# A planner that knows the turns in a product's banks, sums from copies, and another order of 104 products

## The chip, the cores and the metric

The kernel runs on one core of a Trainium2 chip. The metric is the device time of one execution in microseconds (us). The engines that matter are TensorE (PE in the profile, with PEld for its weight loads), VectorE (DVE), ScalarE (ACT) and the queue of SyncE (SP), which issues all DMAs. Each engine works through its own instructions strictly in order and waits for the others at semaphores.

## The reference

Sigmoid attention is followed by a two-layer MLP, all in float32:

```python
scores = scale * (q @ k^T) - log(S)          # batch 8, heads 12, S = 448, head_dim 64
x = merge_heads(sigmoid(scores) @ v)         # 3584 tokens x 768
h = x @ w_in                                 # 768 -> 2048
g = h * sigmoid(1.702 * h)
out = g @ w_out                              # 2048 -> 768
```

The two weight matrices arrive as float64 and are turned into float32 on the chip.

## The kernel before, in words

**Attention.** Two heads make a pair; 24 groups of two pairs are worked through one after the other. TensorE makes the scores (`sc`), ScalarE their sigmoid (`a`), TensorE the product with v (`av`), and `to_x` copies the result (tile `x32`) and stores it to DRAM (`xd`). Beside that, 16 pieces of the weights are decoded (`decode`, tiles `w32`) on VectorE and ScalarE.

**The MLP.** Both layers are computed by a bilinear scheme with 26 products of blocks in place of 32. There are two halves of the tokens (q = 0 and 1) and two layers (m = 0 and 1), so there are 4 x 26 = 104 products. For each one:

- VectorE adds and subtracts blocks of weights (`ws`, `wf`, `kw`) and blocks of x or g (`xs`, `kx`, `gs`, `kg`). These are the sums that the lists `W_SUMS`, `X_SUMS` and `G_SUMS` name.
- Each sum is split in two float32r parts, so that three matmuls give float32 precision. The upper part is a cast that ScalarE or VectorE makes, and the lower part is a subtraction that only VectorE makes (`split_piece` for the weights, tile `w_0` or `w_1`; `pair_of` for x and g, tiles `xp` and `gp`).
- TensorE runs 36 matmuls of 128x128x448 into the four banks of the tile `p{m}_{q}_{r}` (`products`). Products go to the bank groups `h0` and `h1` in turn, so a product's banks must be read out before the product after the next one can start.
- The product is added into up to several sums of products (`Net`): `h` for layer 0 (128 x 1792), `o` for layer 1 (128 x 1344). `Net.add` makes the additions, on VectorE; `Net.copied` makes the first copy of a sum on ScalarE or VectorE. A product can also start from a sum that ScalarE has copied into its banks ahead of the matmuls ("seeded"; `Net.seeds`, in `Net.product`), which saves the addition. ScalarE makes the activation of h (`gelu`).

**The order.** `SEQUENCE` is a table written out by hand: 104 entries (q, m, r). `ways` derives from it and from `AGAIN` how the piece of weights for each product is had: "made" by VectorE, "loaded" again from DRAM (`w<-c`), or the "same" as for one of the last two. `Plan.run` then plays all tasks through with a cost for each, and writes the instructions of every engine in the order in which they begin there. `since` is the time from which a task may begin; `SOON` and `PATIENCE` let an engine wait for a more urgent task; `HORIZON`, `URGENT`, `SPARE` and `KEEP` ration the buffers; `BACKLOG` and `PRESSING` hold DMAs back while the queue is long. These numbers decide only the order of instructions on each engine. On the chip the semaphores decide when they run.

**The turns.** A product's banks may not be read by VectorE and ScalarE at the same time. So where one engine's read stands behind the other's in the program, it waits for a semaphore of the other, although neither needs the other's result. `Plan.run` does not know of these waits.

Of the kernel before, what the change touches and what calls it, by code (L numbers as in the profile page):

```python
# [71 lines left out]
KEEP_FOR = dict(
    w0={0: 6, 1: 25, 2: 25, 3: 3, 4: 3, 5: 12, 6: 3, 7: 6, 8: 12, 9: 3, 10: 12, 13: 3, 14: 25, 15: 6, 16: 25, 17: 6, 18: 25, 19: 6, 20: 12, 21: 12, 22: 12, 24: 12, 25: 25},
    w1={0: 12, 1: 12, 2: 3, 3: 6, 4: 25, 5: 12, 6: 6, 8: 12, 9: 12, 10: 25, 11: 3, 13: 25, 15: 3, 17: 12, 18: 25, 19: 6, 20: 3, 21: 3, 22: 6, 23: 3, 24: 3, 25: 6},
    x0={0: 12, 1: 3, 2: 6, 3: 3, 4: 3, 5: 25, 7: 3, 8: 25, 9: 3, 10: 12, 12: 6, 13: 6, 14: 12, 15: 6, 16: 12, 17: 3, 20: 3, 23: 25, 24: 3},
    x1={0: 25, 1: 3, 2: 12, 3: 6, 5: 6, 6: 6, 7: 6, 8: 12, 10: 25, 11: 25, 12: 12, 13: 6, 14: 25, 15: 12, 16: 12, 17: 6, 18: 3, 19: 6, 20: 6, 21: 12, 22: 3, 24: 6, 25: 3},
    g0={0: 12, 1: 25, 2: 12, 4: 12, 5: 25, 6: 12, 8: 6, 9: 12, 10: 3, 11: 3, 12: 3, 13: 12, 14: 6, 15: 25, 16: 25, 17: 3, 18: 12, 20: 3, 21: 12, 22: 6, 23: 6, 24: 3, 25: 25, 26: 25, 29: 3, 30: 6, 31: 3, 32: 25, 35: 12, 37: 6, 38: 6, 39: 12, 40: 25, 41: 6, 42: 25},
    g1={0: 25, 1: 3, 2: 25, 3: 12, 4: 25, 5: 12, 6: 12, 7: 25, 8: 3, 9: 12, 11: 3, 12: 6, 13: 12, 14: 6, 15: 25, 16: 12, 17: 3, 18: 6, 19: 12, 20: 3, 21: 6, 22: 12, 23: 12, 24: 6, 25: 12, 26: 12, 27: 3, 28: 25, 29: 3, 30: 12, 31: 25, 32: 6, 33: 25, 34: 3, 35: 6, 36: 25, 37: 12, 38: 12, 39: 12, 40: 3, 41: 3, 43: 6},
# [1234 lines left out]
```

## Time and profile before

| | us |
|---|---|
| median of 3 runs (1034.95 to 1041.19) | 1035.44 |
| the profiled execution | 1035.04 |
| its span, first to last instruction | 1033.3 |

| engine | busy us | share of the span | instructions |
|---|---|---|---|
| PE (matmuls) | 1018.3 | 99% | 5588 |
| PEld (weight loads) | 832.3 | 81% | 5588 |
| DVE | 933.0 | 90% | 654 |
| ACT | 588.3 | 57% | 473 |

The granted TensorE clock is 1.0 throughout. The DMAs move 310.63 MB. The busy time of PE overlaps with itself (a matmul begins before the one ahead has ended), so that 99% does not mean that no time is lost there; the lost time is read from the waits and from the distance of the first to the last matmul. In the rows of waits, `DVE h L1262 <- ACT h L1228` says that VectorE's instruction of line 1262 (which writes a tile h) stood idle until ScalarE's instruction of line 1228 was done.

### The profile page before, as it was taken

The page shows a single profiled execution, that of the slowest core. Times are in us where ns is not written, and L with a number is a line of the kernel's source. Part 1 is how long each engine was busy: PE and PEld are TensorE (multiplying, and loading weights), DVE is VectorE, ACT ScalarE, POOL GpSimd, SP SyncE. Part 2 cuts the span into 40 slices and gives each one's busy share as a digit, 9 for nine tenths or more (in the row PEclk, how much of TensorE's full clock was granted, in tenths as well). Part 3 has the DMA queues.
Part 4 walks back from the last instruction along what each step waited for, and adds up shares of the span by engine and source line. Part 5 has one row for each costly group of instructions (what it writes and reads, how often), then busy time and mean ns, then how long its engine had stood idle before and what let it go on. Part 6 is the DMA issues. An engine that isn't in the chain of part 4 may idle for free.

```text
span 1033.3 us, 13713 instructions
## 1 busy us (share of the span) xinstructions
PE 1018.3 (99%) x5588; PEld 832.3 (81%) x5588; DVE 933.0 (90%) x654; ACT 588.3 (57%) x473; POOL 0.2 (0%) x4
## 2 busy tenths in 40 slices
PE   9999999999999999999999999999999999999998
PEld 5545454545898988898899999899999999999987
DVE  6998888897899988998899798999999999999896
ACT  6888887785364455545535444654654336454553
POOL 0000000000000000000000000000000000000000
PEclk9999999999999999999999999999999999999999
DMA  9999998878879868897988885875859389856755
GB/s 351 367 343 383 335 346 317 308 294 308 321 290 379 357 269 292 338 365 286 361 336 312 289 304 202 346 291 195 319 183 382 133 316 367 295 201 240 269 210 223
DMA packets 62799, 310.63 MB, mean 301 GB/s; under 512 B 6544, under 2 KB 14864, under 8 KB 58896
## 3 DMA queue, kind: packets, MB, share of 16 engines
q1 hardware_dynamic: 62736, 309.75, 79.8%
q8 instruction: 44, 0.72, 0.3%
q14 instruction: 19, 0.16, 0.0%
HBM read 200.38 MB, written 109.35 MB: 300 GB/s over the span
## 4 chain that ended last, share of the span: by engine, by line
PE 46%; DVE 4%; ACT 1%; issue 1%; DVEq 0%; ACTq 0%
PE p L845 46%; DVE gp L1052 1%; DVE o L1262 1%; DVE w L813 1%; DVE kg L788 1%; DVE h L1262 0%; ACT p L1186 0%; DVE x L788 0%; DVE h L1229 0%; DVE wf L788 0%; ACT h L1228 0%; ACT o L1228 0%; DVE gp L1041 0%; ACT o L1116 0%; DVEq L813 0%
## 5 line engine op out<-in xcount | busy, mean ns | idle before, releaser
L845 PE MATMUL p<-xp,w 128*128 128x448 f32 x1872 | 387.1, 367 | 8.8 <-DVE xp L1052 3.5
L845 PEld LDWEIGHTS p<-xp,w 128*128 128x128 f32 x1872 | 349.8, 188 | 46.1 <-DVE xp L1052 7.3
L845 PE MATMUL p<-gp,w 128*128 128x448 f32 x1872 | 380.9, 365 | 0.8 <-DVE w L813 0.8
L845 PEld LDWEIGHTS p<-gp,w 128*128 128x128 f32 x1872 | 351.2, 188 | 29.9 <-issue 1.4
L635 ACT ACTIVATE a<-sc,bias 128x896 f32<-128x896 f32 x168 | 156.1, 1014 | 42.9 <-PE sc L665 27.3
L680 PE MATMUL av<-a,vraw 128*64 128x448 f32 x576 | 113.5, 543 | 0.0
L1228 ACT COPY h<-p 128x1792 f32<-128x1792 f32 x30 | 49.7, 1658 | 105.2 <-PE p L845 50.8
L1228 ACT COPY o<-p 128x1344 f32<-128x1344 f32 x37 | 47.2, 1284 | 97.0 <-PE p L845 91.1
L1262 DVE TENSOR_TENSOR h<-h,p 128x1792 f32<-128x1792 f32 x40 | 79.8, 2017 | 20.7 <-ACT h L1228 18.2
L649 PEld LDWEIGHTS sc<-qk 64*128 64x128 f32 x846 | 75.6, 184 | 27.6 <-PE sc L665 16.2
L649 PE MATMUL sc<-qk 64*128 64x448 f32 x846 | 94.6, 373 | 0.8 <-DVE x L710 0.8
L680 PEld LDWEIGHTS av<-a,vraw 128*64 128x64 f32 x576 | 39.2, 137 | 63.2 <-issue 46.9
L1089 ACT ACTIVATE h<-h 128x1792 f32<-128x1792 f32 x28 | 47.4, 1702 | 15.3 <-DVE h L1262 15.3
L1262 DVE TENSOR_TENSOR o<-o,p 128x1344 f32<-128x1344 f32 x34 | 52.2, 1549 | 3.0 <-PE p L845 1.6
L519 DVE TENSOR_TENSOR qk<-qkraw,qk 128x896 fp32r<-128x896 f32 x47 | 50.7, 1089 | 0.6
L1052 DVE TENSOR_TENSOR xp<-x,xp 128x1344 fp32r<-128x1344 f32 x26 | 40.4, 1553 | 7.7 <-ACT xp L1040 7.5
L710 DVE COPY x<-av 128x896 f32<-128x896 f32 x23 | 25.1, 1091 | 17.2 <-PE av L693 17.1
L1052 DVE TENSOR_TENSOR gp<-gs,gp 128x1792 fp32r<-128x1792 f32 x19 | 38.4, 2022 | 1.7 <-ACT gp L1040 1.4
L1052 DVE TENSOR_TENSOR gp<-kg,gp 128x1792 fp32r<-128x1792 f32 x18 | 36.4, 2022 | 1.3 <-ACT gp L1040 1.2
L514 DVE CAST qk<-qkraw 128x896 fp32r<-128x896 f32 x37 | 22.9, 623 | 12.7 <-DMA qkraw<-qk 6.4
L813 DVE TENSOR_TENSOR w<-ws,w 128x1536 fp32r<-128x1536 f32 x19 | 33.3, 1753 | 0.8 <-ACT w L810 0.6
L813 DVE TENSOR_TENSOR w<-kw,w 128x1536 fp32r<-128x1536 f32 x18 | 31.6, 1753 | 2.7 <-ACT w L810 2.6
(109 smaller groups left out, 932.2 us busy)
## 6 DMA issues: line engine op xcount, KB each, us to landing
w<-c SPq DMA_DIRECT2D x34, 768.0 KB, 5.8
w<-w SPq DMA_DIRECT2D x16, 1536.0 KB, 10.5
kg<-kg SPq DMA_DIRECT2D x27, 896.0 KB, 7.0
gl<-g SPq DMA_DIRECT2D x26, 896.0 KB, 7.4
x<-xd SPq DMA_DIRECT2D x34, 672.0 KB, 7.2
c<-w SPq DMA_DIRECT2D x14, 1536.0 KB, 7.3
qkraw<-qk SPq DMA_DIRECT2D x47, 448.0 KB, 7.0
kw<-kw SPq DMA_DIRECT2D x25, 768.0 KB, 7.6
```

What stands on the lines that cost most here:

```text
L514: (costs[1], lambda: nc.vector.tensor_copy(hi(), src())),
L519: lambda: nc.vector.tensor_tensor(lo(), src(), hi().bitcast(F32), op=ALU.subtract),
L635: nc.scalar.activation(a.tile, ps.tile[:, :, :S], AF.Sigmoid, bias=bias, scale=scale)
L649: nc.tensor.matmul(ps.tile[:, j, :S], lhsT=src[kk][rows, S + c * P : S + (c + 1) * P], rhs=src[qq][rows, :S], start=i == 0, stop=i == len( ...
L680: nc.tensor.matmul(ps.tile[cols, n % 2, :S], lhsT=vr.tile[:, at : at + D], rhs=a.tile[:, j], start=c == 0, stop=False, skip_group_check=True,)
L710: (1.09, lambda: nc.vector.tensor_copy(xb.tile, ps.tile[:, :, :S])), [t], [xb, ps], rows)
L813: t_lo = task("DVE", dve(n), lambda: nc.vector.tensor_tensor(into()[:, :, 1], src(), into()[:, :, 0].bitcast(F32), op=ALU.subtract), [t_hi ...
L845: nc.tensor.matmul(ps, lhsT=ws(c // 6)[:, a, c % 6 * P : (c % 6 + 1) * P], rhs=x[:, d, k], start=start and i == 0 and j == 0, stop=stop an ...
L1052: nc.vector.tensor_tensor(part(1)(), node.view(), part(0)().bitcast(F32), op=ALU.subtract)
L1089: t = task("ACT", act(GB), lambda: nc.scalar.activation(view(), node.view(), AF.Gelu_apprx_sigmoid, scale=float(sign)), [*node.done, *(nod ...
L1228: t = on_either((act(self.n), lambda: nc.scalar.copy(view(), node.view())), (dve(self.n), lambda: nc.vector.tensor_copy(view(), node.view())),
L1262: nc.vector.tensor_tensor(view(), x.view(), y.view(), op=ALU.add if s0 == s else ALU.subtract)
```

## The change

It has four parts.

1. `Plan.run` learns of the turns: each task keeps the banks that it reads (`t.banks`), each bank its last reading engine and when that ends, and `since` holds a task back while the other engine reads there.
2. `COPIED` lists products that are copied out of their banks once (on ScalarE or VectorE), after which the additions read the copy.
3. `PLAIN` lists products that are no longer seeded or chained onto a sum in the banks. They begin with an empty bank, and are added by VectorE instead.
4. Another `SEQUENCE`, `AGAIN` and `KEEP_FOR`, and other numbers for the planner.

```diff
-SOON, PATIENCE = 6, 0.8
+SOON, PATIENCE = 4, 0.2
-HORIZON, URGENT, SPARE, KEEP = 14, 4, 1, 2
+HORIZON, URGENT, SPARE, KEEP = 22, 3, 1, 4
-BACKLOG, PRESSING = 6.0, 4
+BACKLOG, PRESSING = 1.0, 4
-ISSUE, LANDING, PER_KB, MM = 0.43, (2.2, 2.5), 0.0027, 0.203
+ISSUE, LANDING, PER_KB, MM = 0.43, (2.2, 3.0), 0.0027, 0.203
 SEQUENCE = (
-    (0, 0, 17), (0, 0, 18), (0, 0, 24), (1, 0, 13), (0, 0, 13), (1, 0, 2), (0, 0, 2), (0, 0, 6),
+    (0, 0, 8), (0, 0, 18), (0, 0, 10), (1, 0, 10), (0, 0, 13), (1, 0, 13), (0, 0, 2), (0, 0, 25),
...
+COPIED = ((0, 1, 2, 4, 6, 8, 13, 14, 16, 17, 18, 20, 21, 22, 23, 24,), ...
+PLAIN = ((0, 3, 5, 6, 8, 12, 13, 15, 16, 19, 21, 24, 25,), ...
...
+        for tag in ("h0", "h1"):
+            for b in self.rings[tag]:
+                for t in b.users if not b.apart else ():
+                    t.banks.append(b)
...
-        def since(t):
+        def since(t, e):
             when = t.ready
+            for b in t.banks:
+                if b.reader not in (None, e):
+                    when = max(when, b.read + SIGNAL)
...
                 free[e] = end - OVERLAP[e]
+                for b in t.banks:
+                    b.reader, b.read = e, max(b.read, end)
...
-                    if c < RANK and len(self.parents[c]) == 1:
+                    if c < RANK and len(self.parents[c]) == 1 and c not in PLAIN[2 * q + m]:
                         away = there(c) - there(before)
...
-                self.arrive(r, (1, node, "psum"))
+                copy = r in COPIED[2 * self.q + self.m] and r not in self.kept and not ps.apart
+                self.arrive(r, (1, self.copied(r, node), "own") if copy else (1, node, "psum"))
```

`COPIED` and `PLAIN` have one tuple for each (q, m), at place 2q + m.

**Where the order moves, first place: the start of the MLP.** In the rows, `p0_0_18` is the product of layer 0, half 0, r = 18; the last number of a name only tells tiles apart; what stands in brackets are the engines and DMA queues that the instruction waits for. VectorE before, from the subtraction that completes the input of the third product (`xp0_25`) on:

```order
L1052 TENSOR_TENSOR xp0_25_2848<-xs0_5_2831,xp0_25_2848 128x1344 [waits PE_49,Activation_49]
L1262 TENSOR_TENSOR h0_26_2817<-h0_26_2817,p0_0_18_2807 128x1792 [waits PE_49]
L1041 CAST xp1_0_2885<-x1_0_2782 128x1344 [waits DMAHW0_49]
L813 TENSOR_TENSOR w_1_2493<-w32_4_2002,w_1_2493 128x2x768 [waits Activation_49]
L1052 TENSOR_TENSOR xp1_0_2885<-x1_0_2782,xp1_0_2885 128x1344 [waits DVE_49]
```

ScalarE before, at the same place:

```order
L1228 COPY h0_26_2817<-p0_0_17_2749 128x1792 [waits DMAHW2_49,DMAHW3_49,DMAHW1_49,DMAHW5_49,DMAHW0_49,DMAHW6_49,DVE_49,DMAHW7_49,PE_49,Activation_49]
L810 CAST w_0_2647<-ws0_4_2819 128x2x768 [waits DVE_49]
L1040 CAST xp0_25_2848<-xs0_5_2831 128x1344 [waits DVE_49]
L1228 COPY h0_8_2873<-p0_0_18_2807 128x1792 [waits DVE_49]
L810 CAST w_1_2493<-w32_4_2002 128x2x768
```

VectorE with the change, from the subtraction that completes the input of the first product (`xp0_11`) to the one for the third (`xp0_8`) and the fourth (`xp1_8`):

```order
L1066 TENSOR_TENSOR xp0_11_2703<-xs0_1_2658,xp0_11_2703 128x1344 [waits DVE_49]
L802 TENSOR_TENSOR xs0_2_2768<-x0_3_2667,x0_7_2696 128x1344 [waits DMAHW5_49,DMAHW3_49,DMAHW6_49,DMAHW1_49,DMAHW7_49,DMAHW0_49,Activation_49]
L802 TENSOR_TENSOR ws0_3_2781<-w32_0_1400,w32_1_1595 128x1536 [waits DVE_49]
L825 CAST w_0_2616<-ws0_2_2685 128x2x768 [waits DMAHW4_49,PE_49]
L827 TENSOR_TENSOR w_0_2616<-ws0_2_2685,w_0_2616 128x2x768 [waits DVE_49]
L1066 TENSOR_TENSOR xp0_8_2804<-xs0_2_2768,xp0_8_2804 128x1344 [waits Activation_49]
L802 TENSOR_TENSOR ws0_4_2829<-w32_4_2009,ws0_3_2781 128x1536 [waits DMAHW5_49,DVE_49]
L825 CAST w_1_2443<-w32_4_2009 128x2x768 [waits PE_49]
L802 TENSOR_TENSOR xs1_1_2854<-x1_3_2770,x1_7_2802 128x1344 [waits DMAHW6_49,DMAHW7_49,DMAHW4_49,DVE_49]
L1055 CAST xp1_8_2865<-xs1_1_2854 128x1344 [waits DVE_49]
L1066 TENSOR_TENSOR xp1_8_2865<-xs1_1_2854,xp1_8_2865 128x1344 [waits DVE_49]
```

ScalarE with the change, at the same place:

```order
L1243 COPY h0_8_2799<-p0_0_8_2733 128x1792 [waits DMAHW4_49,DMAHW3_49,DMAHW5_49,DMAHW0_49,DMAHW6_49,DVE_49,DMAHW7_49,PE_49,Activation_49]
L1054 CAST xp0_8_2804<-xs0_2_2768 128x1344 [waits DVE_49]
L1243 COPY h0_18_2851<-p0_0_18_2789 128x1792 [waits PE_49]
L1243 COPY h0_31_2906<-p0_0_10_2841 128x1792 [waits PE_49]
L1243 COPY h0_0_2912<-p0_0_10_2841 128x1792
```

Before, both engines read the banks of `p0_0_18`: ScalarE's copy waits for VectorE's addition, and the cast of `w_1` stands behind that copy. With the change only ScalarE reads the first three products, and the two casts of weights in this stretch are VectorE's own.

**Second place: product r = 21 of layer 0, half 1.** VectorE before:

```order
L1041 CAST xp1_1_4940<-x1_1_4716 128x1344 [waits PE_49]
L1052 TENSOR_TENSOR xp1_1_4940<-x1_1_4716,xp1_1_4940 128x1344 [waits DVE_49]
L1262 TENSOR_TENSOR h1_6_4844<-h1_6_4844,p0_1_7_4918 128x1792 [waits DMAHW0_49,Activation_49]
L1052 TENSOR_TENSOR xp1_9_4986<-xs1_6_4285,xp1_9_4986 128x1344 [waits Activation_49]
L788 TENSOR_TENSOR ws1_2_4028<-wf13_5009,ws1_2_4028 128x1536 [waits DMAHW5_49]
L1262 TENSOR_TENSOR h1_7_4759<-p0_1_21_4973,h1_7_4759 128x1792 [waits DMAHW7_49,Activation_49]
```

ScalarE before, with the copies of the products r = 7 and r = 21:

```order
L1228 COPY h1_2_4983<-p0_1_7_4918 128x1792 [waits DMAHW5_49,PE_49,Activation_49]
L1040 CAST xp1_9_4986<-xs1_6_4285 128x1344 [waits DVE_49]
L1228 COPY h1_28_5034<-p0_1_21_4973 128x1792 [waits PE_49]
L1228 COPY h1_1_5038<-p0_1_21_4973 128x1792 [waits DMAHW1_49,DVE_49]
L1186 COPY p0_1_25_5052<-h1_36_4383 128x4x448 [waits Activation_49]
```

VectorE with the change, around the same product's additions:

```order
L1066 TENSOR_TENSOR xp1_15_5225<-x1_3_4790,xp1_15_5225 128x1344 [waits Activation_49]
L1277 TENSOR_TENSOR h1_33_4731<-h1_33_4731,h1_34_5071 128x1792 [waits DVE_49]
L802 TENSOR_TENSOR kg1_8_1_5148<-kg1_8_1_5148,gs1_5_5208 128x1792 [waits DMAHW6_49]
L1277 TENSOR_TENSOR h1_34_5071<-h1_34_5071,h1_21_5271 128x1792 [waits DVE_49,Activation_49]
L1066 TENSOR_TENSOR xp1_5_5274<-x1_5_5088,xp1_5_5274 128x1344 [waits DMAHW2_49,PE_49,Activation_49]
L1277 TENSOR_TENSOR h1_19_5024<-h1_19_5024,h1_21_5271 128x1792
```

ScalarE with the change:

```order
L1054 CAST xp1_15_5225<-x1_3_4790 128x1344 [waits Activation_49]
L1243 COPY h1_21_5271<-p0_1_21_5210 128x1792 [waits DVE_49,DMAHW0_49,PE_49,Activation_49]
L1054 CAST xp1_5_5274<-x1_5_5088 128x1344 [waits DMAHW2_49,Activation_49]
L1103 ACTIVATE h1_33_4731<-h1_33_4731 128x1792 [waits DVE_49]
L1054 CAST gp1_31_5321<-kg1_8_1_5148 128x1792 [waits DVE_49,PE_49,Activation_49]
```

Before, VectorE's addition stands between two ScalarE copies of the same banks and takes its turn there. With the change there is one copy, and VectorE's two additions read that copy, which has a buffer of its own.

More of the change, by code (lines that the diff above doesn't have):

```diff
@@ L54 @@
 SEQUENCE = (
[13 rows of a table removed]
-)
-AGAIN = ((1, 5, 8, 11, 13, 17, 21, 24,), (1, 2, 4, 6, 8, 9, 10, 13, 15, 17, 18, 20, 21, 24,))
[13 rows of a table added]
+)
+AGAIN = ((1, 2, 5, 9, 10, 11, 16, 23, 25,), (2, 8, 9, 10, 11, 13, 15, 18, 19, 20, 21, 22, 23, 24,))
+COPIED = ((0, 1, 2, 4, 6, 8, 13, 14, 16, 17, 18, 20, 21, 22, 23, 24,), (0, 1, 2, 4, 5, 8, 10, 14, 15, 16, 18, 19, 21, 22, 23, 24,), (0, 4, 5, 6, 8, 10, 13, 19, 21, 22, 23, 24, 25,), (3, 5, 6, 7, 9, 10, 11, 13, 14, 15, 16, 17, 19, 20, 24, 25,))
+PLAIN = ((0, 3, 5, 6, 8, 12, 13, 15, 16, 19, 21, 24, 25,), (5, 7, 10, 11, 12, 14, 16, 17, 18, 19, 23, 25,), (3, 4, 5, 6, 8, 10, 11, 13, 16, 19, 20, 22, 25,), (0, 2, 5, 7, 9, 14, 18, 24, 25,))
@@ L72 @@
 KEEP_FOR = dict(
[L73 to L76, printed above, removed]
@@ L77 @@
-    g0={0: 12, 1: 25, 2: 12, 4: 12, 5: 25, 6: 12, 8: 6, 9: 12, 10: 3, 11: 3, 12: 3, 13: 12, 14: 6, 15: 25, 16: 25, 17: 3, 18: 12, 20: 3, 21: 12, 22: 6, 23: 6, 24: 3, 25: 25, 26: 25, 29: 3, 30: 6, 31: 3, 32: 25, 35: 12, 37: 6, 38: 6, 39: 12, 40: 25, 41: 6, 42: 25},
-    g1={0: 25, 1: 3, 2: 25, 3: 12, 4: 25, 5: 12, 6: 12, 7: 25, 8: 3, 9: 12, 11: 3, 12: 6, 13: 12, 14: 6, 15: 25, 16: 12, 17: 3, 18: 6, 19: 12, 20: 3, 21: 6, 22: 12, 23: 12, 24: 6, 25: 12, 26: 12, 27: 3, 28: 25, 29: 3, 30: 12, 31: 25, 32: 6, 33: 25, 34: 3, 35: 6, 36: 25, 37: 12, 38: 12, 39: 12, 40: 3, 41: 3, 43: 6},
+    w0={0: 6, 1: 6, 3: 3, 4: 12, 5: 6, 8: 6, 9: 6, 11: 3, 13: 3, 14: 6, 15: 6, 16: 3, 17: 6, 18: 6, 19: 12, 20: 25, 21: 12, 22: 3, 23: 6},
@@ new lines @@
+    w1={1: 3, 2: 3, 3: 6, 4: 6, 5: 25, 7: 12, 8: 25, 9: 3, 10: 6, 13: 25, 14: 6, 15: 12, 16: 12, 17: 12, 18: 12, 19: 3, 20: 3, 21: 3, 22: 3, 25: 3},
+    x0={0: 6, 1: 6, 2: 6, 3: 25, 4: 3, 5: 6, 6: 3, 7: 6, 8: 3, 9: 25, 10: 6, 11: 12, 13: 6, 14: 6, 15: 12, 16: 3, 17: 6, 18: 12, 19: 6, 20: 25, 21: 12, 22: 6, 23: 6, 24: 12, 25: 3},
+    x1={0: 25, 1: 12, 3: 3, 4: 6, 5: 6, 6: 3, 7: 3, 8: 12, 10: 6, 11: 12, 12: 12, 13: 3, 14: 3, 15: 12, 17: 12, 20: 6, 21: 12, 22: 25, 24: 3, 25: 3},
+    g0={0: 12, 1: 3, 2: 12, 4: 25, 5: 6, 6: 12, 7: 12, 8: 6, 9: 6, 10: 3, 11: 12, 12: 25, 14: 6, 15: 3, 17: 12, 18: 12, 19: 3, 20: 12, 21: 3, 22: 25, 23: 25, 24: 3, 25: 12, 26: 3, 27: 6, 28: 25, 29: 6, 30: 3, 31: 25, 32: 3, 33: 12, 35: 3, 36: 12, 37: 25, 40: 3, 42: 12},
@@ L79 @@
+    g1={0: 12, 1: 12, 2: 3, 3: 25, 4: 3, 5: 25, 6: 12, 7: 25, 8: 25, 9: 6, 10: 12, 11: 25, 12: 3, 13: 3, 14: 6, 15: 6, 16: 12, 17: 3, 18: 12, 19: 6, 20: 3, 21: 12, 22: 12, 23: 3, 25: 6, 26: 12, 27: 3, 28: 25, 29: 12, 30: 3, 31: 6, 33: 3, 34: 12, 35: 3, 36: 12, 37: 3, 38: 12, 39: 12, 40: 6, 41: 25, 42: 6, 43: 12},
 )
@@ L98, in __init__ @@
         self.holds, self.landing, self.rate, self.anytime, self.spare = [], LANDING[0], PER_KB, False, 0
+        self.banks = []
 class Buffer:
@@ L103, in __init__ @@
         self.users, self.tile, self.until, self.slot, self.open, self.kind = [], None, 0.0, None, 0, None
-        self.apart = False
+        self.apart, self.reader, self.read = False, None, 0.0
 class Apart:
@@ L242, in run @@
                 if pool:
-                    options.append((max(free[e], min(since(t) for t in pool)), i + 1, e))
+                    options.append((max(free[e], min(since(t, e) for t in pool)), i + 1, e))
             when, _, e = min(options)
@@ L252, in run @@
             else:
-                now = [t for t in pools[e] if since(t) <= when]
+                now = [t for t in pools[e] if since(t, e) <= when]
                 own = [t for t in now if len(t.costs) == 1 or free["ACT"] > when + 1.5]
@@ L257, in run @@
                     c for c in pools[e]
-                    if c.key < min(t.key, doing + SOON) and since(c) < when + PATIENCE * t.costs[e]
+                    if c.key < min(t.key, doing + SOON) and since(c, e) < when + PATIENCE * t.costs[e]
                 ]
@@ L261, in run @@
                     t = min(soon, key=lambda t: t.key)
-                    when = max(when, since(t))
+                    when = max(when, since(t, e))
             t.begun = True
```

24 rows, old and new, of the table SEQUENCE are left out of this document.

## The prediction

> **What bounds the kernel now.** The page's busy times come first.
>
> ```profile
> PE 1018.3 (99%) x5588; PEld 832.3 (81%) x5588; DVE 933.0 (90%) x654; ACT 588.3 (57%) x473; POOL 0.2 (0%) x4
> ```
>
> TensorE looks full and VectorE nearly so. The share can't tell whether TensorE loses time, so I take its timeline (start, length, what, and the idle time before it): the first product, those that begin after the longest stops, and the last; and one stretch of the chain of work without a stop.
>
> ```profile
> 253.25 15.27 PE L845 MATMUL p<-xp,w 128*128 128x448 f32 x74
> 269.17 7.57 PE L845 MATMUL p<-xp,w 128*128 128x448 f32 x36 [0.65 <-DVE xp L1052]
> 277.42 51.35 PE L845 MATMUL p<-xp,w 128*128 128x448 f32 x252 [0.68 <-DVE xp L1052]
> 383.13 30.74 PE L845 MATMUL p<-xp,w 128*128 128x448 f32 x146 [1.69 <-DVE w L813]
> 483.54 22.37 PE L845 MATMUL p<-xp,w 128*128 128x448 f32 x108 [1.02 <-DVE w L813]
> 1007.75 22.12 PE L845 MATMUL p<-gp,w 128*128 128x448 f32 x108 [0.82 <-DVE w L813]
> 648.69 328.94 PE p L845 x1620
> ```
>
> In that stretch 1620 matmuls (45 products) take 328.94 us, 7.31 per product. All 104 would take 760.2. They last from 253.25 to 1007.75 + 22.12 = 1029.87, 776.6 in all, so **16.4 us are lost**. Attention ahead of them takes 253.25, the tail behind them 1033.3 - 1029.87 = 3.4, and the profiled execution stands 1.7 over its span. 253.25 + 760.2 + 16.4 + 3.4 + 1.7 gives its 1035.04 (rounded), 0.4 under the median of the runs. The waits say whom TensorE stopped for:
>
> ```profile
> PE p L845 <- DVE xp L1052: 3.5, 5, 0.7
> PE p L845 <- DVE w L813: 3.5, 3, 1.7
> PE p L845 <- ACT p L1186: 2.0, 2, 1.2
> PE p L845 <- ACT p L1188: 0.3, 1, 0.3
> ```
>
> 9.3 us in 11 stops (total, times, longest): seven for inputs that VectorE finished late, 2.3 for sums that ScalarE copied into the banks. No row waits for a DMA. The other 7.1 are restarts after a stop, which the modelled ends hide, and gaps too short for a row. So VectorE paces TensorE at places, and I look at it in attention and in both parts of the MLP:
>
> ```profile
> 253.00:650.00 397.00, 388.21 (x1882) 351.12 (x1879) 352.75 (x221) 195.08 (x130) 0.00 (x0) 1.00 0.83 313
> 650.00:1022.00 372.00, 371.18 (x1829) 342.92 (x1828) 360.25 (x209) 190.53 (x137) 0.00 (x0) 1.00 0.71 268
> 0.00:253.00 253.00, 251.06 (x1844) 131.31 (x1844) 217.01 (x225) 201.08 (x204) 0.20 (x4) 1.00 0.91 334
> ```
>
> The columns are the stretch, its length, PE, PEld, DVE, ACT and POOL busy, the granted clock, the DMA share and GB/s. From 253 to 1022 VectorE works 713.0 and stands idle 44.3 + 11.7 = 56.0; ScalarE is half idle. What VectorE waits for up to 650, and then behind it:
>
> ```profile
> DVE h L1262 <- ACT h L1228: 21.9, 11, 6.7
> DVE xp L1052 <- ACT xp L1040: 6.5, 3, 2.9
> DVE w L813 <- ACT w L810: 5.5, 4, 2.3
> DVE h L1262 <- PE p L845: 2.9, 5, 1.0
> DVE ws L788 <- DMA kx<-xs: 2.6, 1, 2.6
> DVE h L1229 <- ACT h L1228: 0.7, 1, 0.7
> ...
> DVE gp L1052 <- ACT gp L1040: 3.7, 6, 1.2
> DVE o L1262 <- ACT o L1228: 3.5, 5, 2.2
> DVE gs L788 <- DMA gl<-g: 1.5, 2, 0.8
> ```
>
> Waits behind ScalarE's copies of the same banks (line 1228) are 21.9 + 0.7 + 3.5 = 26.1 in 17 waits. Not all of that is the turn: in the longest, 6.7, ScalarE's copy itself had begun only when the product ended. A copy takes 1.66, so I cap each wait at 1.8 with its signal; about 18 are the turns and 8 are waits for TensorE. Waits for ScalarE's casts are 6.5 + 5.5 + 3.7 = 15.7, those for DMAs about 5 with the shorter ones.
>
> **The change part by part.** *VectorE's work.* I counted both orders from the subtraction that completes the first product's input to the one for the last. Prices are from these groups (times a count | total, mean ns | idle before):
>
> ```profile
> L1262 DVE TENSOR_TENSOR h<-h,p 128x1792 f32<-128x1792 f32 x40 | 79.8, 2017 | 20.7 <-ACT h L1228 18.2 <-PE p L845 2.5
> L1262 DVE TENSOR_TENSOR h<-h,h 128x1792 f32<-128x1792 f32 x8 | 16.1, 2019 | 0.0
> L1262 DVE TENSOR_TENSOR o<-o,o 128x1344 f32<-128x1344 f32 x7 | 10.9, 1552 | 0.0
> L813 DVE TENSOR_TENSOR w<-ws,w 128x1536 fp32r<-128x1536 f32 x19 | 33.3, 1753 | 0.8 <-ACT w L810 0.6
> L1041 DVE CAST gp<-kg 128x1792 fp32r<-128x1792 f32 x4 | 4.3, 1086 | 0.1
> L1041 DVE CAST xp<-x 128x1344 fp32r<-128x1344 f32 x10 | 8.5, 854 | 0.5 <-PE p L845 0.5
> L811 DVE CAST w<-kw 128x1536 fp32r<-128x1536 f32 x3 | 2.9, 955 | 0.0
> L1229 DVE COPY h<-p 128x1792 f32<-128x1792 f32 x5 | 10.1, 2023 | 1.1 <-ACT h L1228 0.7 <-PE p L845 0.3
> L1228 ACT COPY h<-p 128x1792 f32<-128x1792 f32 x30 | 49.7, 1658 | 105.2 <-PE p L845 50.8 <-DVE h L1262 35.3 <-DMA xd<-x 11.4
> ```
>
> Additions and subtractions of 1792 go from 169 to 174 (+5 x 2.02 = 10.1), of 1344 from 127 to 135 (+8 x 1.55 = 12.4), of 1536 from 88 to 90 (+3.5). Casts of 1344 go from 15 to 20 (+4.3), of 1536 from 10 to 15 (+4.8), of 1792 from 11 to 3 (-8.7). Copies of 1792 go from 5 to 1 (-8.1), two smaller ones go (-2.7). That is +15.6, less 0.06 for each of 11 more instructions, since neighbours overlap by that much (740.0 of durations stand for 713.1 of time): **+14.9**, so 728. TensorE's 103 products to that point take 752.9. VectorE has 25 us to be idle in, where it was idle 56.
>
> An addition costs the same from a bank (2017 ns) as from a copy (2019), so reading copies is priced at nothing. The Trainium skill ("Perfetto Trace Analysis", Optimizing Scalar/DVE Operations) gives VectorE about 125 ns of access overhead on PSUM and about 60 on SBUF; by that, the 38 additions that leave the banks (92 to 54) would save an estimated 2.5 us more. The two groups' means differ by 2 ns the other way, so the row decides.
>
> *The turns.* Products that both engines read fall from 39 to 12 in the orders. At the same mean, 18 us of turns become 5.5.
>
> *The casts.* A cast that ScalarE makes (up to 1.7 us) needs other work on VectorE between the source's last sum and the subtraction that reads the cast. Summing durations in between, 25 of 84 such casts had under 2.2 us before; with the change 1 of 85 has, and the next has 3.2. I take the 15.7 us as 0.5. The cover is gone where ScalarE itself is held up by more than a product's time.
>
> *Seeds.* ScalarE's copies into the banks go from 40 to 27, so 2.3 us of TensorE's stops become about 1.6. ScalarE's own work falls by 10 us in the MLP; with half its time free that is worth nothing.
>
> *The start.* Rows of SP, ScalarE and VectorE, and one of DMAs (KB, us to landing):
>
> ```profile
> 254.51 0.32 SPq L487 DMA_DIRECT2D xd<-x  x1
> 261.09 1.66 ACT L1228 COPY h<-p 128x1792 f32<-128x1792 f32 x1 [11.37 <-DMA xd<-x]
> 267.57 1.55 DVE L1052 TENSOR_TENSOR xp<-xs,xp 128x1344 fp32r<-128x1344 f32 x1
> x<-xd SPq DMA_DIRECT2D x34, 672.0 KB, 7.2
> ```
>
> The first buffers in what was attention's space wait for attention's last store, to 261.1. In the new order `xs0_2` is such a one and stands right behind the first product's input, so VectorE stops there. From 261 on it needs 1.55 + 1.75 + 0.95 + 1.75 + 1.55, less overlaps, and completes the third product's input (`xp0_8`) at 268.2, due at 253.25 + 2 x 7.31 = 267.9: 0.3 lost. Before, that came at 269.1 and the fourth product's cast behind a turned copy was late too: 0.65 + 0.68 idle there and the restarts, 1.9 lost.
>
> *Where it is tight.* Behind that point VectorE has 44.3 us of work to the ninth product's input and reaches it at 268.2 + 44.3 = 312.5. To that comes 0.8 of waiting for `x1_7`, whose load follows the release of a buffer by `ws0_3` at 264.4 and takes 7.2, to 271.6, where VectorE would be at 270.8. That makes 313.3, due at 311.7 + 0.3: 1.3 more lost. From the 15th to the 41st product it has 187.7 of work for 190.1 of TensorE's time (182.3 before), from the 54th to the last 359.5 for 365.5 (355.4 before). So it can't get ahead. Up to the 28th product, where the orders leave it 4.6 us of idling (TensorE's time with the 1.6 lost, less VectorE's work), what it idles beyond that is lost again. I expect 4.4 there (three of the 12 turns 1.4, DMAs 2, the rest 1), which just fits.
>
> *Loads.* DMAs go from 409 to 406, bytes up by 2.6 of 310 MB. `BACKLOG` 1.0 issues what isn't pressing later, and pieces loaded again go from 17 to 20; SP's queue is passed by other DMAs, but no TensorE wait for a DMA shows now. Price nothing, up to the rival below. Attention keeps TensorE's order and its 253.25.
>
> Sum of what stays lost: 0.3 + 1.3 at the start, 1.6 for seeds, 0.8 for a late w as the one at 1007.75, 2 of short gaps, and 0.5 for one turn in a tight place, 6.5. 16.4 - 6.5 = 9.9, so the profiled execution comes to 1025.1 and the median to **1025.5**.
>
> **The rivals.**
>
> - *All of it goes.* VectorE's 25 us of room hide every wait and only the short gaps stay: 16.4 - 2 = 14.4 saved, **1021**. For it: 5.5 + 0.5 + 5 and some 5 unnamed are 16. Against it: the room is not at the start.
> - *Copies wait instead.* Additions that read a ScalarE copy go from 53 to 98; each needs the product's end, ScalarE's turn and 1.66. If 45 of them wait 0.4 more, VectorE idles 16 + 18 = 34 beside its 728: 762 against 713 + 55 = 768, so 6 saved, and at 37 idle 3: **1029 to 1032.5**. ScalarE's copies wait themselves now (105.2 us in the group of 30), which speaks for it; that most of them stand two or more products ahead of their additions speaks against it.
> - *Loads come late* (slower). A loaded piece can begin only when TensorE has left the tile two pieces before, and must land within one product:
>
> ```profile
> w<-c SPq DMA_DIRECT2D x34, 768.0 KB, 5.8
> SPq L487 <- PE p L845: 116.4, 32, 18.7
> ```
>
>   5.8 of 7.31 leaves 1.5. If SP stands 2.5 behind another wait (it has waited up to 18.7), each of 20 pieces stops TensorE for 1.0: +20 - 9.9, **1045.5**; it turns slower from 2.0 behind. No such stop in 17 pieces speaks against it.
> - *The turns stay in another place*, and VectorE idles 56 as before: +14.9, **1050**. From 41 idle it is slower. That 39 products became 12 speaks against it.
>
> **How the numbers follow.** A measurement of this kernel tells about 1% from no change, here 10.4 us. Forecast (1022.5 to 1028.5) 0.60, all goes 0.14, copies wait 0.16, late loads 0.06, turns stay 0.04. The forecast's middle lies 0.4 above the 1% line (1025.1), so 0.28 of its 0.60 count as faster: with 0.14 that is 0.42. Slower is 0.06 + 0.04 and 0.01 of the copies. The range runs from 1020.5 to 1033, through the first three cases.
>
> **What would show it.** VectorE busy 728 between the first and last product's inputs, and its rows behind ScalarE's line of `copied` down from 26 to under 10, those behind casts near 1; TensorE's stops down to about 4 us, the first at some 268 and 312; products after 330 nearly without a stop. Wrong would make it TensorE rows that wait for a DMA, or additions of `h<-h,h` that idle behind copies.

## The result, and the profile after

The changed kernel takes a median of **1021.36 us** (20 runs, 1018.21 to 1034.12); the kernel before, on the same chips, 1038.22 us (20 runs, 1034.27 to 1043.42). The ratio is **0.9855, 95% interval 0.9827 to 0.9882**. The 20 runs stand in two groups, 13 from 1018.2 to 1024.0 and 7 from 1032.6 to 1034.1; the ratio leaves most of the upper group out (by the means of all runs, 1025.1 and 1038.0, it is 0.988), and the profiled execution (1034.12, span 1032.3) belongs to it, so that its total can't be read against the one of before without the section on the two cadences below.

The busy times of the page, TensorE's timeline from the first to the last product, and its only row of waits inside the products:

```profile
PE 1024.7 (99%) x5588; PEld 833.3 (81%) x5588; DVE 941.8 (91%) x657; ACT 586.6 (57%) x471; POOL 0.2 (0%) x4
```

```profile
254.64 59.25 PE L859 MATMUL p<-xp,w 128*128 128x448 f32 x290
314.61 133.93 PE L859 MATMUL p<-xp,w 128*128 128x448 f32 x646 [0.73 <-DVE xp L1066]
...
664.14 364.72 PE L859 MATMUL p<-gp,w 128*128 128x448 f32 x1764
```

```profile
PE p L859 <- DVE xp L1066: 0.7, 1, 0.7
```

Of 11 stops with 9.3 us one is left, of 0.7. Counted from the distances between the starts of matmuls (what is over 0.203 us in those above 0.28), 14.4 us were lost before and 2.0 now. VectorE by stretch (columns as before), and what it waits for from 253 to 1022:

```profile
253.00:650.00 397.00, 396.06 (x1926) 358.86 (x1923) 369.18 (x234) 190.59 (x127) 0.00 (x0) 1.00 0.87 321
650.00:1022.00 372.00, 372.00 (x1802) 337.84 (x1801) 359.51 (x207) 183.31 (x130) 0.00 (x0) 1.00 0.73 270
```

```profile
DVE xs L802 <- DMA xd<-x: 8.6, 1, 8.6
DVE w L825 <- PE p L859: 6.6, 4, 2.5
DVE h L1277 <- PE p L859: 5.5, 5, 4.0
DVE xp L1055 <- PE p L859: 4.3, 6, 1.8
DVE gp L1066 <- ACT gp L1054: 3.3, 3, 2.8
DVE w L827 <- ACT w L824: 2.7, 5, 1.1
...
DVE o L1277 <- ACT o L1243: 1.0, 3, 0.5
```

Lines 1243 (ScalarE) and 1244 (VectorE) are the copies out of a product's banks, 1277 the additions, 1054, 1055 and 824, 825 the casts, 1066 and 827 the subtractions. The waits behind ScalarE's copies, 26.1 us before, are 1.0; those behind its casts, 15.7 before, 6.0. What stands ahead of them now, but for the 8.6 us until attention's last store has landed, are waits for TensorE: VectorE is early. In this execution TensorE ran at the slower of two cadences (next paragraph), which gives VectorE time; in the run with 64 columns below, at the faster one, the waits behind ScalarE's copies and casts are 0.4 and 3.7. VectorE's work is 369.18 + 359.51 = 728.7, where 713.0 stood. The additions by their source:

```profile
L1277 DVE TENSOR_TENSOR h<-h,h 128x1792 f32<-128x1792 f32 x37 | 74.3, 2020 | 0.3
L1277 DVE TENSOR_TENSOR h<-h,p 128x1792 f32<-128x1792 f32 x24 | 48.1, 2017 | 5.8 <-PE p L859 5.5
```

**Two cadences.** One stretch of the chain of waits, from 344.54 to the end of the products, holds 3310 matmuls without any stop:

```profile
344.54 684.34 PE p L859 x3310
```

That is 0.2067 us a matmul. In the chain of before, 1620 took 328.94, 0.2031. In both the granted clock is 1.0. The starts of single matmuls, averaged over 20, show two cadences, 0.2027 and 0.2067 us from start to start, and nothing in between; in these two traces TensorE keeps one until something interrupts it. In the profile of before 3020 matmuls of products run at the faster and 674 at the slower one, changing only at stops; in this profile 426 and 3308. The 0.004 us over all 3744 make 15 us. That is the distance from the fastest run (1018.2) to the mean of the upper group (1033.3); the means of the two groups lie 12.7 apart.

### The profile page after: what moved, and what is told of

Its sections match the earlier page's. It is cut to its first block, busy times and chain, and to the rows that moved or that the text cites. A ratio compares the mean times of both kernels' runs of the same rounds, so it can differ in the third digit from the quotient of the medians.

```text
span 1032.3 us, 13705 instructions
## 1 busy us (share of the span) xinstructions
PE 1024.7 (99%) x5588; PEld 833.3 (81%) x5588; DVE 941.8 (91%) x657; ACT 586.6 (57%) x471; POOL 0.2 (0%) x4
## 4 chain that ended last, share of the span: by engine, by line
PE 87%; DVE 6%; DMA 4%; issue 2%; ACT 0%; SPq 0%; DVEq 0%; ACTq 0%
PE p L859 66%; PE av L694 10%; PE sc L663 8%; PE sc L679 2%; PE av L707 2%; DMA qkraw<-qk 1%; DVE xs L802 1%; DMA w<-w 1%; DVE xp L1066 1%; DMA x<-xd 1%; DMA kw<-ws 1%; DVE w L827 1%; DMA xd<-x 0%; DVE h L1277 0%; DVE w L825 0%
## 5 line engine op out<-in xcount | busy, mean ns | idle before, releaser
L859 PE MATMUL p<-gp,w 128*128 128x448 f32 x1872 | 387.4, 368 | 0.0
L1243 ACT COPY h<-p 128x1792 f32<-128x1792 f32 x34 | 56.1, 1658 | 107.4 <-PE p L859 102.6
L1243 ACT COPY o<-p 128x1344 f32<-128x1344 f32 x40 | 51.2, 1280 | 89.3 <-PE p L859 83.8
L1277 DVE TENSOR_TENSOR h<-h,h 128x1792 f32<-128x1792 f32 x37 | 74.3, 2020 | 0.3
L1054 ACT CAST gp<-kg 128x1792 fp32r<-128x1792 f32 x22 | 37.3, 1697 | 53.1 <-PE p L859 46.9
L1277 DVE TENSOR_TENSOR h<-h,p 128x1792 f32<-128x1792 f32 x24 | 48.1, 2017 | 5.8 <-PE p L859 5.5
L1277 DVE TENSOR_TENSOR o<-o,o 128x1344 f32<-128x1344 f32 x30 | 46.3, 1553 | 1.1 <-ACT o L1243 1.0
L1066 DVE TENSOR_TENSOR gp<-kg,gp 128x1792 fp32r<-128x1792 f32 x22 | 44.4, 2019 | 3.0 <-ACT gp L1054 2.8
L724 DVE COPY x<-av 128x896 f32<-128x896 f32 x18 | 19.7, 1092 | 21.4 <-PE av L707 21.1
L824 ACT CAST w<-kw 128x1536 fp32r<-128x1536 f32 x14 | 20.7, 1482 | 30.1 <-PE p L859 30.1
```

The costliest lines, as they stand in the source:

```text
L824: t_hi = on_either((act(n), lambda: nc.scalar.copy(into()[:, :, 0], src())), (cast(n), lambda: nc.vector.tensor_copy(into()[:, :, 0], src())),
L859: nc.tensor.matmul(ps, lhsT=ws(c // 6)[:, a, c % 6 * P : (c % 6 + 1) * P], rhs=x[:, d, k], start=start and i == 0 and j == 0, stop=stop an ...
L1054: t_hi = on_either((act(n), lambda: nc.scalar.copy(part(0)(), node.view())), (cast(n), lambda: nc.vector.tensor_copy(part(0)(), node.view())),
L1066: nc.vector.tensor_tensor(part(1)(), node.view(), part(0)().bitcast(F32), op=ALU.subtract)
L1243: t = on_either((act(self.n), lambda: nc.scalar.copy(view(), node.view())), (dve(self.n), lambda: nc.vector.tensor_copy(view(), node.view())),
L1277: nc.vector.tensor_tensor(view(), x.view(), y.view(), op=ALU.add if s0 == s else ALU.subtract)
```

## The experiments

Each ran beside runs of the kernel before on the same chip: 1036.63 us (15 runs) for the first four, 1037.43 (24) for the next four, 1036.99 (17) for the last four. "Lost" is counted from the starts of matmuls as above.

**The change once more**, unaltered.

> The changed kernel once more, unaltered, for a profile in which each product takes the 7.31 us of before. Theory V (VectorE's waits were what stopped TensorE, and they are gone): about 1021, 0.9855 of before; TensorE's waits inside the products under 2 us in all, one of them at about 313; VectorE idle 25 to 30 us from the first product on, most of it behind TensorE and not behind ScalarE. Theory S (the gain sits in attention or the tail): first product earlier than 251 us or a tail under 2.5 us.

Measured: 1018.19, 1018.56, 1031.78, 1034.08, 1034.45 and 1034.56, a median of 1032.93; ratio 0.9856 (0.9803 to 0.991), again without most of the upper group. The profiled execution was of the upper group again, and its chain shows why:

```profile
255.24 773.96 PE p L859 x3744
```

All 104 products without one stop, at 0.2067 us a matmul. The upper group is no kernel that waits, but the slower cadence from the first product on.

**The planner's knowledge of the turns alone**: the kernel before with part 1 of the change, its old order of products and old numbers, `COPIED` and `PLAIN` empty.

```diff
-        def since(t):
+        def since(t, e):
             when = t.ready
+            for b in t.banks:
+                if b.reader not in (None, e):
+                    when = max(when, b.read + SIGNAL)
```

> Before, with the planner's knowledge of the turns alone: old sequence, old numbers, no copies, nothing plain. In the order 35 products are read by both engines (39 before, 12 with the whole change), and VectorE's work from first to last product is 721.9 us (713.1 before). Theory K (knowing the turns is what helps): at least half of the gain, 1028 or less. Theory V (waits have to leave the order, and it hardly changes): 1033 to 1040, no clear gain.

Measured: 1048.17 (6 runs), ratio **1.011** (1.0081 to 1.014), slower, beyond both. The waits of VectorE do what they should, its total behind ScalarE's copies falls from 26.1 to 3.3:

```profile
DVE h L1277 <- PE p L859: 15.5, 15, 5.6
DVE gp L1066 <- ACT gp L1054: 10.0, 14, 2.5
...
DVE h L1277 <- ACT h L1243: 2.3, 3, 0.8
```

But TensorE lost 27.6 us. Its waits, and the longest with the instructions of VectorE, ScalarE and TensorE that make it:

```profile
PE p L859 <- ACT p L1200: 14.0, 3, 9.5
```

```profile
651.76 2.02 DVE L1244 COPY h<-p 128x1792 f32<-128x1792 f32 x1 [0.25 <-ACT p L1200]
653.82 1.66 ACT L1200 COPY p<-h 128x1792 f32<-128x1792 f32 x1 [0.46 <-DVE h L1244]
655.53 9.76 PE L859 MATMUL p<-xp,w 128*128 128x448 f32 x37 [9.48 <-ACT p L1200]
```

Line 1200 copies a sum into the banks ahead of a seeded product. It waits for VectorE's copy of a sum out of banks (line 1244), which begins at 651.76, 5.7 us after TensorE's last matmul ended (646.05). With the turns gone, other work stands late.

**The change without that knowledge.**

```diff
-                if b.reader not in (None, e):
+                if False and b.reader not in (None, e):
```

> The changed kernel with the planner's knowledge of the turns taken out again; sequence, copies, plain products and numbers stay. 13 products are read by both engines (12 with it); VectorE's work is 731.3 (728.0), and between the 15th and 41st product TensorE's time is at one point only 4.9 us ahead of VectorE's work (10.7). Theory K: most of the gain is lost, over 1030. Theory V: only what the tighter stretch costs, 2 to 6 us, 1023 to 1027.

Measured: 1034.64 (10 runs), ratio 0.9971 (0.9953 to 0.9989). Most of the gain is gone, as Theory K had it, and the range of 1023 to 1027 missed. 9.5 us are lost, the largest part in one place, again behind a copy out of banks (VectorE, then TensorE):

```profile
389.35 0.85 DVE L1055 CAST xp<-x 128x1344 fp32r<-128x1344 f32 x1
391.12 2.02 DVE L1244 COPY h<-p 128x1792 f32<-128x1792 f32 x1 [0.92 <-DMA g<-h]
393.29 6.91 PE L859 MATMUL p<-xp,w 128*128 128x448 f32 x19 [4.25 <-DVE h L1244]
```

**`COPIED` only for layer 0 of half 0**: the other three of its four tuples emptied, all else as in the change.

```diff
-COPIED = ((0, 1, 2, 4, ...), (0, 1, 2, 4, ...), (0, 4, 5, 6, ...), (3, 5, 6, 7, ...))
+COPIED = ((0, 1, 2, 4, ...), (), (), ())
```

> The changed kernel with copies only in layer 0 of the first half; the other three lists of copies are empty. 24 products are read by both engines (12), ScalarE's casts keep their cover (6 of 85 under 2.2 us), VectorE's work is 736.8 (728.0). Theory V: turns come back for half of the 27 products that had lost them, and VectorE's room shrinks by 9 us: 1028 to 1034, with 5 to 10 us of VectorE's idle time behind ScalarE's copies. Rival (copies do nothing, the sequence does it all): 1021 to 1024.

Measured: 1080.36 (6 runs), ratio 1.0415 (1.0388 to 1.0441), far beyond the ranges given. 55.2 us are lost; the two longest rows of TensorE's waits, and the place of the longest stop (VectorE, ScalarE, TensorE):

```profile
PE p L859 <- DVE xp L1055: 16.6, 2, 10.7
PE p L859 <- DVE h L1244: 15.2, 4, 6.5
```

```profile
314.02 1.76 DVE L827 TENSOR_TENSOR w<-ws,w 128x1536 fp32r<-128x1536 f32 x1 [5.60 <-ACT w L824]
312.52 1.47 ACT L824 CAST w<-ws 128x1536 fp32r<-128x1536 f32 x1 [6.27 <-PE p L859]
323.19 1.08 PE L859 MATMUL p<-xp,w 128*128 128x448 f32 x2 [10.71 <-DVE xp L1055]
```

VectorE stands for a cast of weights whose tile TensorE frees only at 312.5, and behind it in VectorE's order lie four sums of x, a cast and a subtraction that TensorE needs for its next product. With fewer copies the planner orders these differently. The table of 104 products fits only the copies that it was found with.

**More work for VectorE**, in the kernel before and in the changed one, order untouched.

```diff
+    pad = const.tile([P, 192], F32, name="pad")
...
+                nc.vector.memset(pad, 0.0)
                 if sign > 0:
                     nc.vector.tensor_tensor(part(1)(), node.view(), part(0)().bitcast(F32), op=ALU.subtract)
```

> The kernel before with one more VectorE instruction ahead of each subtraction that completes an input of x or g (104 times a memset of 128x192, an estimated 0.2 us each by the 1.1 us that a cast of 1792 elements takes, so some 20 us in all); everything else stands in the same order. Theory of the room: VectorE was idle 56 us in the MLP, and TensorE's stops stand where VectorE is late, so that part of the 20 us goes straight into the stops: 8 to 18 us slower, 1045 to 1055 against some 1037. Rival, TensorE's cadence alone: VectorE's work is hidden, and the time moves by less than 3 us.

> The changed kernel with the same 104 memsets of 128x192 (some 20 us more work for VectorE). Theory of the room: 25 us of room take most of it, but not at the tight places (2.4 us from the 15th to the 41st product, against 27 x 0.2 = 5.4; 6 us from the 54th on, against 10): 5 to 9 us slower than the change without it, 1026 to 1031 in the runs that are at 1018 without it, and stops behind VectorE's subtractions for inputs come back. Rival, TensorE's cadence alone: no more than 2 us slower and no stop. Rival, VectorE is already at its limit: the whole 20 us are seen.

The memsets in the kernel before, and TensorE's two largest rows of waits there:

```profile
L1052 DVE MEMSET pad<- 128x192 f32 x103 | 22.5, 218 | 0.0
```

```profile
PE p L846 <- DVE xp L1054: 4.5, 6, 0.9
PE p L846 <- DVE w L814: 4.4, 4, 1.8
```

Measured before: 1040.62 (12 runs), ratio 1.0034 (1.0017 to 1.005), so 3 us for 22.5 us of work, where 8 to 18 were expected. A miss: VectorE's 56 us of idle time in the kernel before do take up most of the work. The cadence was not held here. The profiled execution, the slowest of the 12 (1043.94), has 1455 matmuls at the slower cadence, 781 more than before (3 us), and loses 20.1 us by the starts against 14.4, so the stops alone grew by 5.7 there. Measured after: 1032.54 (10 runs, 1024.27 to 1036.06), outside the expected 1026 to 1031, but a mixture of cadences that can't be priced; in its profile, at the slower one, no stop is above 0.4 us. It was run again with the cadence held, below.

**The change's `SOON` and `PATIENCE` alone**, in the kernel before.

```diff
-SOON, PATIENCE = 6, 0.8
+SOON, PATIENCE = 4, 0.2
```

> The kernel before with the change's SOON and PATIENCE (4 and 0.2) and nothing else of it. In its order 9 of 87 ScalarE casts have under 2.2 us of cover on VectorE, before 25 of 84; the turns stay (39 products read by both engines). Theory of parts: VectorE's waits behind casts fall from 15.7 to about 6, those behind copies stay near 26; 2 to 6 us faster than before, 1031 to 1035. Rival, only the whole order counts: other stops come up for those that go, and it is not faster than before, 1036 to 1045.

Measured: 1048.17 (6 runs), ratio **1.0106** (1.0081 to 1.0131), slower, as the rival had it, and beyond its 1045. VectorE's waits, and TensorE's largest row:

```profile
DVE h L1262 <- ACT h L1228: 28.2, 13, 6.6
DVE o L1262 <- ACT o L1228: 10.2, 8, 3.7
DVE o L1229 <- ACT o L1228: 6.5, 3, 4.6
...
DVE gp L1052 <- ACT gp L1040: 2.6, 5, 1.0
```

```profile
PE p L845 <- DVE w L813: 6.8, 8, 2.0
```

The casts' waits fall from 15.7 to 3.4, below the 6 worked out from the order; those behind copies of the same banks (line 1228) rise from 26.1 to 47.8, and 24.9 us are lost.

**Both, still without the tables**: the kernel before with the knowledge of the turns and the two numbers (the two diffs above together).

> The kernel before with the planner's knowledge of the turns and with SOON 4 and PATIENCE 0.2, with the old order of products, the old other numbers, and no COPIED or PLAIN. Either of the two alone made it slower by 1.1%: the knowledge alone put seeds late (14.0 us of stops behind ScalarE's copies into banks), the numbers alone took waits behind casts from 15.7 to 3.4 us but raised those behind copies of the same banks from 26 to 48. Theory that the two are needed together and the tables do little: the turns and the casts both go, 1022 to 1030. Rival, the two do not help as long as most of the products are read by both engines and 40 are seeded: 1036 to 1048, and VectorE's waits behind ScalarE fall while TensorE's stops for seeds and inputs stay.

Measured: 1043.57 (6 runs), ratio 1.0074 (1.0048 to 1.01), slower, by the rival. VectorE's waits, its stretch and TensorE's largest row:

```profile
DVE xp L1055 <- PE p L859: 12.0, 7, 4.8
DVE w L825 <- PE p L859: 9.1, 7, 2.5
```

```profile
253.00:1030.00 777.00, 763.82 (x3713) 698.33 (x3710) 720.37 (x444) 363.60 (x250) 0.00 (x0) 0.99 0.77 288
```

```profile
PE p L859 <- ACT p L1202: 3.9, 2, 2.1
```

No wait behind ScalarE's copies is left and about 5 us behind its casts, and yet VectorE stands idle 777 - 720.4 = 56.6 us, as before: now 34 of it for products and tiles that TensorE has not finished, and 14 for DMAs. 21.1 us are lost, 3.9 of them behind ScalarE's negated seeds (line 1202).

**One irregular matmul ahead of products**, in the changed kernel, of eight widths in turn.

```diff
+        if brk and start:
+            n, (c, k), (a, d) = SIZES[len(breaks) % len(SIZES)], todo[0], TERMS[0]
+            nc.tensor.matmul(ps[:, :n], lhsT=ws(c // 6)[:, a, ...], rhs=x[:, d, k][:, :n], start=True, stop=False, ...)
         for i, (c, k) in enumerate(todo):
```

> The changed kernel with one more matmul ahead of each product that begins with an empty bank (77 of 104): into the same bank, with the same weights and the first 32, 64, 96, 128, 192, 256, 320 or 384 columns of the same block, the sizes taking turns; the product's own first matmul overwrites it, so nothing else changes and no wait is added. The work is 77 x some 0.09 us = 7 us more. TensorE's matmuls follow each other in one of two cadences, 0.2027 or 0.2067 us, and so far they changed only at stops. Theory that any irregular matmul draws the cadence anew: each run has a mixture of both after the 77 short matmuls, the runs lie closer together than those of the change itself (within 6 us, some 1028 to 1034), and if the size decides, each size has one cadence behind it. Rival, only a stop draws it anew: one cadence throughout, and two clusters of times 13 to 16 us apart, at some 1025 and 1040.

Measured: 1031.91 (7 runs, 1030.38 to 1034.61), one group. 73 of the 77 short matmuls are in the trace (some records are missing), and the cadence behind each is one of the two. By width, how many were followed by which:

```
columns      32  64  96  128  192  256  320  384
faster        7   9   7    6    6    6    6    6
slower        3   0   2    3    3    3    3    3
```

From 192 columns on all 36 keep the cadence that was there ahead of them. Narrower ones may change it, with no wait. From the slower cadence all seven matmuls of 32 to 128 columns led to the faster one, two of them with 64 columns. From the faster, 32, 96 and 128 columns led to the slower in 8 of 23 cases, 64 columns in none of 7.

**A matmul of 64 columns at a few places**: the same in 15 products of the changed kernel, in every second product with empty banks of the kernel before, and in the changed kernel with the memsets.

```diff
+            if n in range(8, 14) or n % 8 == 0:
+                nc.tensor.matmul(ps[:, :64], ..., rhs=x[:, d, k][:, :64], start=True, stop=False, ...)
```

> The changed kernel with a matmul of 64 columns ahead of the 1st, the 9th to the 14th and then every eighth of the 77 products that begin with an empty bank (15 in all; the product's first matmul overwrites what it writes). In the run with short matmuls of eight sizes, the nine of 64 columns were followed by the faster cadence (0.2027 us) nine times of nine, also behind the slower one. One costs 0.028 + 0.285 - 0.203 = 0.11 us, 1.65 in all. Theory that 64 columns set the cadence: all runs at 1018.2 + 1.7, 1019 to 1022, without a second cluster, and 0.983 of before. Rival, nine of nine was luck (six of nine would be the share of the other sizes): two clusters as without it, or runs in between at 1022 to 1032.

> The kernel before with a matmul of 64 columns ahead of every second product that begins with an empty bank (32 x 0.11 = 3.5 us). Theory: before draws its cadence anew at each of some 25 stops and has the slower one for a quarter of the time (a quarter of 15 us = 4); with the faster one set again and again the two cancel, the median stays within 3 us of before (1034 to 1040), the runs lie closer together than the 10 us of before, and its stops stay. The distance of the changed kernel to before at one cadence would then be 15 to 18 us. Rival: the stops of before come from something that the cadence sets, and it becomes faster by more than 5 us.

> The changed kernel with both additions: 102 memsets of 128x192 on VectorE (22.2 us by their trace) and the 15 matmuls of 64 columns. In the run with the memsets alone the profiled execution had the slower cadence throughout, in which TensorE gives VectorE 15 us more room, and no stop over 0.4 us. Theory of the room, now at the faster cadence: 25 us of room less 22 leave the tight places short: 4 to 9 us slower than the steady kernel without memsets, 1024 to 1029. Rival, VectorE has more room than the orders give: under 2 us slower, 1019 to 1022.

Measured for the changed kernel: **1021.87** (4 runs, 1020.14 to 1022.42), ratio 0.9852 (0.9825 to 0.9878): no second group. In its trace 3687 matmuls run at the faster cadence and 33 at the slower. TensorE's timeline (the first short matmul, the only stop with a wait of its own, the last row) and a piece of the chain, 0.2028 us a matmul:

```profile
253.95 0.30 PE L863 MATMUL p<-xp,w 128*128 128x64 f32 x1
...
314.03 29.43 PE L869 MATMUL p<-xp,w 128*128 128x448 f32 x142 [0.74 <-DVE xp L1076]
...
972.55 44.02 PE L869 MATMUL p<-gp,w 128*128 128x448 f32 x216
```

```profile
717.03 109.51 PE p L869 x540
```

This version is 3.7 us slower than the best run of the change (1018.2) and 11 faster than its upper group (1033.3 on average); by the mean of all runs it takes 1021.6 against 1025.1 of the change's 20. Four runs alone would show little, since 15 of the 26 runs of the change were of the lower group; the trace shows the cadence, and the six runs with the memsets, below, form one group too.

The kernel before: 1038.74 (12 runs, 1036.17 to 1041.98), ratio 1.0016 (1.0001 to 1.0032). The slower cadence falls from 674 matmuls to about 300, the stops stay (VectorE, TensorE):

```profile
DVE h L1272 <- ACT h L1238: 21.8, 11, 6.7
```

```profile
PE p L855 <- DVE xp L1062: 3.3, 5, 0.7
```

Taking off the short matmuls (3.5 and 1.65 us), the change is worth 1035.2 - 1020.2 = **15.0 us** by the medians at nearly one cadence. By the two profiled executions, 1036.40 and 1021.82, it is 1032.9 - 1020.2 = 12.7, and the 250 more matmuls at the slower cadence in the kernel before are 1.0 of that.

The changed kernel with the memsets: 1026.4 (6 runs, 1024.46 to 1028.93), 4.5 above the one without them, inside the 4 to 9 (by the two profiled executions, 1024.81 and 1021.82, 3.0). Small stops for inputs come back near 828 and 909 (and at 798):

```profile
828.13 0.27 PE L864 MATMUL p<-gp,w 128*128 128x64 f32 x1 [0.18 <-DVE w L828]
...
909.40 65.52 PE L870 MATMUL p<-gp,w 128*128 128x448 f32 x322 [0.15 <-DVE gp L1078]
```

From the 15th to the 41st product, the first of the two tight places, only one stop came, near 453, of about 0.25 us by the starts.

## Why the prediction was right, and where it was not

**The time.** 1025.5 was forecast and 1021.36 measured, inside the range. The rival "all of it goes", 1021 by 16.4 - 2 = 14.4 saved, is nearer to what happened: by the starts the loss went from 14.4 to 2.0, and at nearly one cadence the change is worth 12.7 to 15.0. That the median lay inside the range has luck in it, since TensorE's cadence decides it: in the six runs of the change once more it was 1032.93, at the range's very end. The forecast's 6.5 us that would stay lost is the sum that failed, term by term:

- *The start.* `xp0_8` was forecast for 268.2 and its subtraction ended at 266.53 + 1.55 = 268.08; the wait ahead of it is the attention store, 8.6. It cost nothing, not 0.3, since the first product began at 254.64 and not at 253.25: attention did not keep its time (253.6 to 255.2 in the traces of the changed order with all its parts, 252.8 to 253.3 in three of the old one). The 1.3 lost at 312.5 to 313.3 came as 1.2, at 313 to 315, in the profile of the change and in the one with 64 columns. The place was right; the size has luck in it. In the profile of the change the ninth product was due 1.0 later than forecast (254.64 + 8 x 7.30 = 313.0), and VectorE completed its input 1.3 later (314.56 in place of 313.3), after waiting 1.6 in place of 0.8 and working 0.6 longer.
- *Seeds, 1.6.* No stop behind lines 1200 and 1202 is left. Counting 27 copies at the mean cost of 40 was wrong: before, the 2.3 us came from three places, not from each copy.
- *A late w, 0.8, and a turn, 0.5.* Neither came.
- *Short gaps, 2.* They were taken for a fixed toll of TensorE. In the run of the change without a stop 0.1 us are lost in all. Of the 16.4 lost before, 14.4 stand in distances above 0.28 us, at stops; of the other 2.0, 1.2 are what the two cadences differ from the chain's mean, and 0.6 a dozen distances of 0.21 to 0.28.

**VectorE's work.** Forecast 728 from 713 + 14.9; 728.7 in the profile of the change, 728.15 from 253 to 1012 in the one with 64 columns. Reading copies costs what reading banks costs: 2020 and 2017 ns. By the figures of the Trainium skill ("Perfetto Trace Analysis", Optimizing Scalar/DVE Operations), about 125 ns of access overhead for VectorE on PSUM and about 60 on SBUF, reading copies would be an estimated 2.5 us cheaper; these rows show nothing of it.

**The room.** 25 us were worked out, with the tight places inside it. 22.2 us of more work cost 4.5 (3.0 by the profiles) at the faster cadence: there was that room, and not all of it where it was needed. The stops came back in the second of the two tight places, from the 54th product on, and hardly in the first. That holds for the changed kernel. The same reading failed for the kernel before, where 22.5 us cost 3 and not 8 to 18.

**The turns and the casts.** Their waits fell from 26.1 to 1.0 and from 15.7 to 6.0 (forecast 5.5 for the turns alone, 0.5 for the casts). The step that failed is the one that turned these waits into TensorE's time. The kernel before with both parts of the planner has none of the first and about 5 us of the second, and is 7 us slower. VectorE's idle time then stands elsewhere, 56.6 us of it: the rival "the turns stay in another place" is what happens without the new tables. A wait of VectorE is a cost only if the input behind it is late for TensorE, and that is a matter of the whole order. The new order of products was not run with the old planner, nor `PLAIN` or `AGAIN` by themselves, so what each of the tables brings stays open; shown is that the order with the planner's knowledge gains, that without it most is lost, and that with fewer copies the kernel is 44 us slower than before.

**The product's 7.31 us.** The sum took 760.2 for 104 products as given. By the two cadences it is 758.9 or 773.8. That the profile of before held both (its chain gave 0.2031, a mean of them) was not seen, and a loss that 11 of the 26 runs of the change show is as large as the gain. Before, any of some 25 interruptions can change the cadence (six did in its trace), so that its runs lie within some 9 us; with the stops gone, one draw can last for the whole MLP, as it did in the run of the change once more.

**Loads** as priced: no TensorE row waits for a DMA after the change. **Copies wait instead** did not come: the 37 additions `h<-h,h` idle 0.3 us in all.

## What to carry to other kernels

The sum of an engine's waits is no price: follow each to the input of the bound engine that is late behind it, and expect that a planner which removes one kind of wait moves the idle time to the next. A table found together with a planner's rules is to be judged with them, since the two parts of the planner that were tried without the tables made this kernel slower, each alone and both together. And look at the distance of the starts of matmuls before a difference of 1 or 2% is put down to waits: here two cadences at one granted clock were worth as much as the change.

## What the runs showed of the hardware

- **Two cadences of TensorE at granted clock 1.0.** For matmuls of 128x128x448 in float32r, 0.2027 or 0.2067 us from start to start. It stayed the same over all 3744 matmuls of one trace. A stop, or a matmul of 128 columns or fewer, can change it, but neither is needed: five changes in three traces have no distance above 0.21 us at them, each at the first or second matmul of a product (at 455.3 in the kernel before with memsets, at 1023.9 in the one with 64 columns, at 332.4, 431.7 and 873.7 in the one with both parts of the planner). Behind 64 columns it was the faster one in 9 of 9 cases of the run with eight widths, and in 58 of 60 of the three later runs; in the other two a distance of 0.27 or 0.32 us follows two or three matmuls behind. What sets the cadence is open; only the widths above were tried.
- **A long stop costs more than itself.** After the stop of 9.48 us in the run with the knowledge of the turns alone, the stretch from 656 to 660 (columns as before; the clock is the 0.51):

```profile
656.00:660.00 4.00, 4.00 (x12) 3.57 (x12) 3.59 (x2) 2.31 (x2) 0.00 (x0) 0.51 0.76 263
```

  Twelve matmuls start in 4 us (0.373 us apart, against 0.203), for about a dozen matmuls: some 2 us on top. After the stop of 4.25 us in the change without that knowledge sixteen matmuls ran so. Shorter stops may or may not do it: in the run with the knowledge alone eight or nine matmuls ran so after distances of 2.12 and 2.37 us from start to start, in the kernel before with both parts of the planner none after 2.18 and 2.50.
